# Expert 0 loaded earlier, its splits kept in the projection tiles, and routing in two nearly equal parts

## The chip, the core and the metric

The kernel runs on one core of one Trainium2 chip. The metric is the time of one execution in microseconds (us), as the device takes it. The engines are named as in the profile: PE (TensorE, matrix products), DVE (VectorE), ACT (ScalarE), POOL (GpSimd), and SP, whose queue issues most transfers.

## The reference

Four batches (B) of 576 tokens (S), 8 heads of 64, 512 model columns (DM), 1024 inner columns (FF), 8 experts. It is cut to what is computed:

```python
# attention: each query sees the 64 keys up to itself
scores = where((rel >= 0) & (rel < 64), scale * (q @ k.T), -1e9)
x = softmax(scores) @ v
# gated FFN: projection, a 3-tap filter along the tokens, projection
h = maximum(x @ w_in, 0.0)
conv_out[t] = sum(conv_w[k] * h[t + k - 1] for k in range(3))
x = (h * sigmoid(conv_out)) @ w_out
# mixture of experts, one expert per token
logits = x @ w_gate
local_gate = sigmoid(x @ w_local)
for b, s:
    e = argmax(logits[b, s]) if s == 0 or local_gate[b, s] < 0.5 else prev_e
    p = softmax(logits[b, s])
    out[b, s] = p[e] * (maximum(x[b, s] @ w1[e], 0.0) @ w2[e])
```

A token thus keeps the expert of the token ahead of it when its local gate says so.

## The kernel before

**Exact products.** fp32 data is held as a high and a low part (names ending in H and L, or h and l), and each product is three PE matmuls: high x high, high x low, low x high. The high part is a copy by ACT (`cast`), the low part a subtraction (`rest_of`) on DVE, or on POOL for slot 0.

**Phase 1, the batches.** For each batch `ffn(b)` goes through eight feature tiles (f0 to f7) of 128 columns. 24 matmuls per tile (L345) are evacuated by ACT into `hb`; the filter and gate (L361 to L371) run on POOL, DVE and ACT and leave `gH` and `gL`, the gated features, in a ring. Then `ffn_out(i)` (L384) multiplies each tile of 128 tokens with `wout` (24 matmuls of 512 columns) and stores `y` through SP's queue. The attention of the next batch is mixed between these steps by `mix`, and `share(b)` says how many of its steps may have run after a given number of FFN steps. In this phase a scheduler sets the order of the engines' instructions from a timing model; nothing is reordered by hand.

**The transition.** The last batch's tiles are numbered 13 to 17 (I0 = 13, NT = 18). From `logits_ahead` on, the order of PE, DVE and ACT is written out. `logits_ahead` computes the gate logits of tiles 13 to 17 straight from gH and gL (48 PE matmuls L453 into `psG`, two per feature tile and product), `gate` and `route` find each token's expert, and its rank among that expert's tokens (PE steps L630, L639, L645, L656 to L664, each a round trip to DVE), and `A` is the one-hot matrix of the rank. `slots_of` turns that into slots of 128 tokens of one expert: DVE's products `bm` (L695 to L702), PE's L706, the token indices `gidx`, and the output weights `pslot` (POOL's products `bp` at L745, PE's L749, DVE's reduction L750). `tail()` yields one output matmul at a time, and `ahead(n)` puts n of them (fillers) at a place in the order. Tiles 0 to 12 have been routed in batch 3 already.

**Phase 2, the slots.** 23 slots run without condition, two more under one. Slot t has a gather, `X` (4 transpositions), `MM1` (24 matmuls, L890), `HT` (8 transpositions), `MM2` (24 matmuls, L920), and a scatter of rows from `osb` to `out`. Expert weights come as raw tiles `raw1` and `raw2` (4 each, 512 KB a tile), are split by ACT and DVE (L836, L842), and a load is skipped where the expert stays. Slot 0's x stays on the chip: `X0` takes it from `psX`, which L414 fills. In this kernel the raw tiles and the split tiles (pools `ws`, `ws2`) take the space that `win`, `x` and `h` leave when phase 1 closes, so expert 0's loads (L795, L797) begin after the last L345.

Of the kernel before, what the change touches and what calls it, by code (L numbers as in the profile page):

```python
# [21 lines left out]
def kernel(  # L22
# [29 lines left out]
    RING = 640  # L52
    scale = 1.0 / float(D) ** 0.5
# [39 lines left out]
    if True:  # L93
# [6 lines left out]
        hb = [h_p.tile([P, S + 2], F32, name=f"hb{i}", bufs=1) for i in range(2)]  # L100
# [146 lines left out]
        def stage_AV(b, hp, g):  # L247
            if (b, hp, g) == (b, 0, 0):
                xT[b] = []
            if g == 0:  # L250
                xT[b].append((x_p.tile([P, S], F32R, name="xH"), x_p.tile([P, S], F32R, name="xL")))
# [71 lines left out]
        def ffn(b):  # L323
# [3 lines left out]
            for f in range(KF):  # L327
                if b == 0:
                    if cin:
                        fin.append(conv_in(*cin.pop(0)))  # L330
                        if len(fin) > 1:
                            fin.pop(0)()
                    fin.append(conv_out(f))
                    if f:
                        fin.pop(0)()
# [18 lines left out]
                t = h_p.tile([P, S], F32, name="t", bufs=3)  # L354
# [189 lines left out]
        I0 = (B - 1) * S // P  # L544
        gidx = const.tile([P, TS], I32, name="gidx")
# [15 lines left out]
        def route_init():  # L561
# [4 lines left out]
            def iota(shape, pattern, base, mult, name):  # L566
                ti = r1.tile(shape, I32, name=name + "_i")
# [27 lines left out]
            tl("ohc", [P, NT - I0, E], BF16)  # L595
# [29 lines left out]
        def route(i0, i1):  # L625
# [47 lines left out]
            if i0 == 0:  # L673
                s_ = r1.tile([P, E], F32, name="ohs")
                nc.vector.tensor_reduce(s_, oh.rearrange("p i e -> p e i"), axis=AX.X, op=ALU.add)
                nc.vector.tensor_copy(rt["ohc"], s_.unsqueeze(1).to_broadcast([P, NT - i1, E]))
            nc.vector.tensor_tensor(
                rt["A"][:, g], rl.unsqueeze(2).to_broadcast([P, n, P]), rt["i128"].unsqueeze(1).to_broadcast([P, n, P]), op=ALU.is_equal
            )

        def slots_of():
# [109 lines left out]
    x0_p = ctx.enter_context(tc.tile_pool(name="x0", bufs=1, side="right"))
    raw1 = [raw_p.tile([P, FF], F32, name=f"raw1_{kk}") for kk in range(KD)]
    raw2 = [raw_p.tile([P, 2, DM], F32, name=f"raw2_{kk}") for kk in range(KD)]
    for kk in range(KD):
        nc.sync.dma_start(out=raw1[kk], in_=w1[0, kk * P:(kk + 1) * P, :])  # L795
    for kk in range(KD):
        nc.sync.dma_start(out=raw2[kk], in_=w2[0, kk * 2 * P:(kk + 1) * 2 * P, :].rearrange("(j p) d -> p j d", p=P))  # L797
# [3 lines left out]
    KORD = (3, 0, 1, 2)  # L801
# [10 lines left out]
    def load1(t):  # L812
        for kk in KORD:
# [4 lines left out]
                cond=c,  # L818
# [91 lines left out]
    def MM2(t):  # L910
# [11 lines left out]
        o = s2.tile([P, DM], F32, name="osb")  # L922
# [6 lines left out]
    def start(t):  # L929
        load1(t)  # L930
# [4 lines left out]
    def run(t0, t1):  # L935
# [4 lines left out]
        if t0 + 1 < t1:  # L940
            gather(t0 + 1)
            load1(t0 + 1)
            load2(t0 + 1)
            if t0 == 0:
                split(raw1, w1s, "a", 1, KORD[0:1])
                X0(rt["psX"], 1)
# [56 lines left out]
    with tc.manual_schedule(engines={mybir.EngineType.PE, mybir.EngineType.DVE, mybir.EngineType.Activation}):  # L1003
# [31 lines left out]
        for _ in rest:  # L1035
            pass
# [43 lines left out]
```

## Time and profile before

| | |
|---|---|
| three timed runs | 681.88, 684.84, 686.81 us (median 684.84) |
| the profiled execution | 680.33 us |
| its span | 678.5 us |
| PE busy | 639.7 us, 94% |
| DVE busy | 515.2 us, 76% |
| ACT busy | 449.7 us, 66% |
| POOL busy | 205.2 us, 30% |
| mean granted clock | 0.967 |

The span is the time from the first to the last instruction of the profiled execution. About the first 140 us hold the attention and FFN of batch 0 with the conversion of the weights; batches 1 to 3 run to 335, the transition to 384, the slots to 671, and the last scatter to the end. In the rows, a window is a stretch of the span with the busy time of each engine in it and the number of instructions; the granted clock is 1.00 for 2.4 GHz and 0.50 for 1.2 GHz. In a timeline row the bracket tells how long the engine waited before the instruction, and for what.

### The profile page before, as it was taken

The page shows a single profiled execution, that of the slowest core. Times are in us where ns is not written, and L with a number is a line of the kernel's source. Part 1 is how long each engine was busy: PE and PEld are TensorE (multiplying, and loading weights), DVE is VectorE, ACT ScalarE, POOL GpSimd, SP SyncE. Part 2 cuts the span into 40 slices and gives each one's busy share as a digit, 9 for nine tenths or more (in the row PEclk, how much of TensorE's full clock was granted, in tenths as well). Part 3 has the DMA queues.
Part 4 walks back from the last instruction along what each step waited for, and adds up shares of the span by engine and source line. Part 5 has one row for each costly group of instructions (what it writes and reads, how often), then busy time and mean ns, then how long its engine had stood idle before and what let it go on. Part 6 is the DMA issues. An engine that isn't in the chain of part 4 may idle for free.

```text
span 678.5 us, 13033 instructions
## 1 busy us (share of the span) xinstructions
PE 639.7 (94%) x4379; PEld 555.0 (82%) x4379; DVE 515.2 (76%) x1054; ACT 449.7 (66%) x972; POOL 205.2 (30%) x223
## 2 busy tenths in 40 slices
PE   5688897999999999999979999999999999999994
PEld 4468787899999999999847878888888888888883
DVE  4877999726893467825968659989899899899982
ACT  3575755636784467623433468898889888988972
POOL 5553565301541023432757421121111211211101
PEclk9788999899999999999969999999999999999998
DMA  7867350342234202010141246611451444412760
GB/s 164 210 168 185 95 128 32 76 120 67 68 67 102 79 32 53 12 63 32 60 188 47 64 152 223 241 60 34 156 178 37 165 158 156 161 42 83 238 257 12
DMA packets 91880, 75.75 MB, mean 112 GB/s; under 512 B 72266, under 2 KB 72290, under 8 KB 91812
## 3 DMA queue, kind: packets, MB, share of 16 engines
q1 hardware_dynamic: 87040, 64.11, 31.7%
q0 software_dynamic: 3680, 10.75, 4.7%
q8 instruction: 35, 0.57, 0.4%
q14 instruction: 33, 0.27, 0.1%
q10 hardware_dynamic: 1092, 0.04, 0.1%
HBM read 127.84 MB, written 11.27 MB: 205 GB/s over the span
## 4 chain that ended last, share of the span: by engine, by line
PE 39%; issue 31%; DMA 14%; DVE 11%; POOL 2%; ACT 2%; SPq 1%; POOLq 0%; DVEq 0%; ACTq 0%
PE psM L345 12%; PE psO L384 12%; DMA out_dram<-osb,sidx 10%; PE psA L195 3%; PE psA L261 3%; PE psA L238 2%; POOL xg L861 2%; PE psA L166 2%; DMA raw<-in_moe_w_in_dram 1%; DVE t L362 1%; PE psA L198 1%; DVE lf L469 1%; DVE t L363 1%; DVE lf L467 1%; DMA raw<-in_moe_w_dram 1%
## 5 line engine op out<-in xcount | busy, mean ns | idle before, releaser
L842 DVE TENSOR_TENSOR aL<-raw,aH 128x1024 fp32r<-128x1024 f32 x88 | 102.0, 1220 | 12.0 <-ACT aH L836 12.0
L842 DVE TENSOR_TENSOR bL<-raw,bH 128x1024 fp32r<-128x1024 f32 x84 | 97.3, 1220 | 3.6 <-ACT bH L836 0.9
L924 POOL DMA_INDIRECT out_dram<-osb,sidx x23 | 23.3, 1015 | 231.6 <-ACT osb L923 224.3
L836 ACT ACTIVATE aH<-raw 128x1024 fp32r<-128x1024 f32 x92 | 90.1, 1062 | 0.6 <-DVE gL L371 0.6
L836 ACT ACTIVATE bH<-raw 128x1024 fp32r<-128x1024 f32 x88 | 86.3, 1067 | 0.0
L345 PE MATMUL psM<-xH,winH 128*128 128x288 f32 x256 | 79.8, 312 | 0.1
L345 PE MATMUL psM<-xL,winH 128*128 128x288 f32 x256 | 77.3, 302 | 0.0
L345 PE MATMUL psM<-xH,winL 128*128 128x288 f32 x256 | 76.4, 299 | 0.0
L371 POOL TENSOR_TENSOR gL<-t,gH 128x576 fp32r<-128x576 f32 (+6 forms) x54 | 57.5, 1074 | 57.7 <-ACT gH L370 57.7
L920 PE MATMUL psO<-bH,hh 128*128 128x512 f32 x184 | 74.0, 402 | 0.4 <-ACT hh L907 0.4
L920 PE MATMUL psO<-bL,hh 128*128 128x512 f32 x184 | 72.3, 393 | 0.5 <-DVE bL L842 0.5
L920 PE MATMUL psO<-bH,hl 128*128 128x512 f32 x184 | 72.4, 393 | 0.0
L890 PE MATMUL psH<-aH,xh 128*128 128x512 f32 x176 | 70.9, 403 | 0.0
L890 PE MATMUL psH<-aH,xl 128*128 128x512 f32 x176 | 69.3, 394 | 0.0
L890 PE MATMUL psH<-aL,xh 128*128 128x512 f32 x176 | 69.2, 393 | 0.0
L384 PE MATMUL psO<-woutH,gH 128*128 128x262 f32 (+2 forms) x240 | 63.4, 311 | 1.4 <-ACT gH L370 1.4
L361 POOL TENSOR_SCALAR t<-hb,cw 128x576 f32<-128x576 f32 x31 | 30.4, 980 | 113.2 <-ACT hb L352 100.2
L384 PE MATMUL psO<-woutH,gL 128*128 128x262 f32 (+2 forms) x240 | 62.4, 307 | 0.9 <-POOL gL L371 0.9
L384 PE MATMUL psO<-woutL,gH 128*128 128x262 f32 (+2 forms) x240 | 63.1, 307 | 0.0
L213 ACT ACTIVATE sS<-sS,mx 128x128 f32<-128x128 f32 (+1 forms) x144 | 55.2, 387 | 11.1 <-DVE mx L205 10.9
L345 PEld LDWEIGHTS psM<-xH,winH 128*128 128x128 f32 x256 | 49.0, 191 | 1.0 <-ACT hb L352 0.4
L345 PEld LDWEIGHTS psM<-xL,winH 128*128 128x128 f32 x256 | 48.9, 191 | 0.3
(281 smaller groups left out, 1498.5 us busy)
## 6 DMA issues: line engine op xcount, KB each, us to landing
raw<-in_moe_w_dram SPq DMA_DIRECT2D x180, 512.0 KB
v<-in_v_dram SPq DMA_DIRECT2D x56, 128.0 KB
y_dram<-ysb SPq DMA_DIRECT2D x18, 256.0 KB
kt<-in_k_dram SPq DMA_DIRECT2D x32, 128.0 KB
qt<-in_q_dram SPq DMA_DIRECT2D x32, 128.0 KB
raw<-in_moe_w_in_dram SPq DMA_DIRECT2D x8, 512.0 KB
raw<-in_moe_w_out_dram SPq DMA_DIRECT2D x8, 512.0 KB
raw2e<-in_moe_w_dram SPq DMA_DIRECT2D x4, 512.0 KB
```

The costliest lines, as they stand in the source:

```text
L195: nc.tensor.matmul(ps[:, j * P + lo:(j + 1) * P], qbd[:, c, :], kT[:, k0:W * (c + 1)], start=True, stop=True)
L213: nc.scalar.activation(sS[:, c, lo:P], sS[:, c, lo:P], AF.Exp, scale=-1.0, bias=mx[:, c:c + 1], accum_out=sume[:, c:c + 1],)
L261: nc.tensor.matmul(ps[64 * h:64 * h + 64, W * j:W * j + W], vt[:, h, :], a[0:kk, j, 64 * h:64 * h + 64], start=True, stop=True,)
L345: nc.tensor.matmul(ps[:, 0:HS], wt[:, kk, f * P:(f + 1) * P], xt[:, c0:c0 + HS], start=n == 0, stop=n == 3 * KD - 1,)
L361: e1.tensor_scalar(tt, h1, cw[:, 1, f:f + 1], 0.0, op0=ALU.mult, op1=ALU.add)
L371: e1.tensor_tensor(gL[:, f, r:r + m], t[:, done:done + m], gH[:, f, r:r + m].bitcast(F32), op=ALU.subtract)
L384: nc.tensor.matmul(p_[:, 0:cs.stop - cs.start], gt[:, kk, r:r + P], wt[:, kk, cs], start=n == 0, stop=n == 3 * KF - 1,)
L836: nc.scalar.activation(H_, raws[kk], AF.Copy)
L842: eng.tensor_tensor(L_, raws[kk], H_.bitcast(F32), op=ALU.subtract)
L890: nc.tensor.matmul(ps, a, w[:, g * DM:(g + 1) * DM], start=n == 0, stop=n == 3 * KD - 1)
L920: nc.tensor.matmul(ps, a[:, kk], w[:, kk % 2, :], start=n == 0, stop=n == 3 * KF - 1)
L924: nc.gpsimd.indirect_dma_start(out=out[:, :], out_offset=bass.IndirectOffsetOnAxis(ap=sidx[:, t:t + 1].bitcast(U32), axis=0), in_=o, in_of ...
```

## The change

- `win`, `wout`, `x`, `h` and the ring are kept for the whole kernel. The split weights of the slots live in them by turns: even slots in `win` and `x` (and an end of the ring), odd slots in `wout` and the ring. The pools `ws`, `ws2`, `x0` and the second output buffer `osb` are gone; the staging of a slot's output is `o_v`, one view of `h`. The space so freed takes `raw1` and `raw2`, and expert 0 is loaded at the start of batch 3.
- Tiles 0 to 8 (R0 = 9) are routed at that point, 9 to 17 in the transition (before: 0 to 12 and 13 to 17). The gate of tiles 9 to 12 is computed when the FFN of batch 3 comes to f = 5.
- Slot 0's low parts are made by DVE, behind the index operations of `slots_of`. `norm` and `chosen` (parts of `slots_of` before) run in steps of `route`.
- The fillers have new numbers, and `tail()` first takes tiles 13 and 14 in turn.
- `share(b)` spreads the attention of batches 2 and 3 over 28 steps, 16 of them in the FFN's matmuls.
- At the end HT(22) moves into MM2(21), and the last raw weights use `raw1`.

The core of the diff:

```diff
 def tail():
-    for i in range(I0, NT):
+    first = [ffn_out(i, False, 1) for i in (I0, I0 + 1)]
+    for g in first:
+        for _ in range(3 * (KF - 1)):
+            yield next(g)
+    for g in first:
+        yield from g
+    for i in range(I0 + 2, NT):
...
-        for n in (4, 2, 2, 2, 0):
+        for n in (22, 6, 2, 1, 0):
             next(lg, None)
             ahead(n)
-        split(raw1, w1s, "a", 0, KORD[0:2])
         gate(I0, NT)
-        ahead(8)
-        ks = list(KORD[2:])
-        for _ in route(I0, NT):
-            ahead(5)
-            if ks:
-                split(raw1, w1s, "a", 0, (ks.pop(0),))
         gate_exp(I0, NT)
+        ahead(7)
+        for _, n, f in zip(route(R0, NT), (4, 2, 3), (None, norm, chosen)):
+            if f:
+                f()
+            ahead(n)
         sl = slots_of()
         next(sl)
-        split(raw1, w1s, "a", 0, ks)
         for kk in KORD:
-            ahead(12)
+            ahead(9)
+            cast(raw1, w1s, "a", 0, kk)
+        ahead(2)
+        next(sl)
+        next(sl)
+        for kk in KORD[0:3]:
             cast(raw2, w2s, "b", 0, kk)
-        ahead(12)
-        next(sl)
-        for kk in KORD:
-            rest_of(raw2, w2s, 0, kk)
-        ahead(7)
-        next(sl, None)
+        for kk in KORD[0:3]:
+            rest_of(raw1, w1s, 0, kk)
+        ahead(14)
+        rest_of(raw1, w1s, 0, KORD[3])
         for _ in rest:
             pass
+        X0(rt["psX"], 1)
+        next(sl, None)
...
 def rest_of(raws, store, t, kk):
-    eng = nc.vector if t else nc.gpsimd
-    eng.tensor_tensor(L_, raws[kk], H_.bitcast(F32), op=ALU.subtract)
+    nc.vector.tensor_tensor(L_, raws[kk], H_.bitcast(F32), op=ALU.subtract)
...
 def ffn(b):
             for f in range(KF):
+                if b == B - 1 and f == 5:
+                    gate(R0, I0)
+                    gate_exp(0, I0)
...
 def share(b):
-    n1, n2, na = 4 * KF, 4 * (4 + b % 2), 34
-    if b == 0:
-        return lambda m: 16 * m // n1 if m <= n1 else 16 + (na - 16) * (m - n1) // n2
-    return lambda m: na * m // (n1 + n2)
+    n1, n2, na = 4 * KF, 4 * (4 + b % 2), 34 if b == 0 else 28
+    return lambda m: 16 * m // n1 if m <= n1 else 16 + (na - 16) * (m - n1) // n2
...
 # in run(t0, t1)
+                    split(end2, w2s, "b", t, KORD[0:2])
+                    MM2(t - 1, {8: lambda: HT(t)})
+                    split(end2, w2s, "b", t, KORD[2:4])
```

On DVE the end of batch 3's FFN stands as follows before; the L361 to L365 are the filter's steps of f6 and f7 (f7 in two parts), and A is the first routing part's one-hot matrix.

```order
L668 TENSOR_TENSOR rk<-psR,oh 128x104
L669 TENSOR_REDUCE rf<-rk 128x13
L670 CAST ri<-rf 128x13
L365 SCALAR_TENSOR_TENSOR t<-t,hb_132 128x576
L671 TENSOR_SCALAR rl<-ri 128x13
L672 TENSOR_SCALAR rh<-ri 128x13
L362 SCALAR_TENSOR_TENSOR t<-hb_131,cw,t 128x576
L677 TENSOR_TENSOR A<-rl,i_4053 128x1664
L363 SCALAR_TENSOR_TENSOR t<-hb_131,cw,t 128x576
L361 TENSOR_SCALAR t<-hb_132,cw 128x287
L361 TENSOR_SCALAR t<-hb_132,cw 128x289
```

And on DVE now (the steps have the numbers L370 to L374, and `t` and `hb` are views of h):

```order
L682 TENSOR_SCALAR rh<-ri 128x9
L693 TENSOR_TENSOR A<-rl,i_4017 128x1152
L374 SCALAR_TENSOR_TENSOR h<-h 128x576
L371 SCALAR_TENSOR_TENSOR h<-h,cw 128x576
L372 SCALAR_TENSOR_TENSOR h<-h,cw 128x576
L374 SCALAR_TENSOR_TENSOR h<-h 128x576
L371 SCALAR_TENSOR_TENSOR h<-h,cw 128x576
L372 SCALAR_TENSOR_TENSOR h<-h,cw 128x576
L374 SCALAR_TENSOR_TENSOR h<-h 128x576
L371 SCALAR_TENSOR_TENSOR h<-h,cw 128x576
L372 SCALAR_TENSOR_TENSOR h<-h,cw 128x576
L370 TENSOR_SCALAR h<-h,cw 128x287
```

`A` now has three whole feature tiles between it and the first step of f7 (128x287).

On PE, from the transposition of `key` to the ranks (L384, now L393, are the fillers), before:

```order
L630 MATMUL psR<-ident,key 18x128
L384 MATMUL psO<-woutH,gH 128x512
L384 MATMUL psO<-woutL,gH 128x512
L384 MATMUL psO<-woutH,gL 128x512
L384 MATMUL psO<-woutH,gH 128x512
L384 MATMUL psO<-woutL,gH 128x512
L639 MATMUL psR<-dg,ltri 18x18
L384 MATMUL psO<-woutH,gL 128x512
L384 MATMUL psO<-woutH,gH 128x512
```

and on PE now:

```order
L640 MATMUL psR<-ident,key 18x128
L393 MATMUL psO<-woutH,gL 128x512
L393 MATMUL psO<-woutH,gH 128x512
L393 MATMUL psO<-woutL,gH 128x512
L393 MATMUL psO<-woutH,gL 128x512
L649 MATMUL psR<-dg,ltri 18x18
L393 MATMUL psO<-woutH,gH 128x512
L393 MATMUL psO<-woutL,gH 128x512
L655 MATMUL psR<-ident,cm 128x18
L393 MATMUL psO<-woutH,gL 128x512
L393 MATMUL psO<-woutH,gH 128x512
L393 MATMUL psO<-woutL,gH 128x512
```

Four fillers stand behind L640 where five stood, two behind L649 where five stood, and three before the ranks where five stood.

## Rows read from the trace of the kernel before

**Rows 1.** The page's 40 slices of the span: TensorE busy, and its clock.

```profile
PE   5688897999999999999979999999999999999994
...
PEclk9788999899999999999969999999999999999998
```

**Rows 2.** Windows of the transition: from:to, length, busy by engine, clock, DMA share, GB/s.

```profile
338.87:354.25 15.38, 11.75 (x37) 6.89 (x36) 10.54 (x23) 6.06 (x11) 9.03 (x5) 0.67 0.57 217
354.25:384.00 29.75, 29.47 (x203) 24.64 (x203) 22.75 (x54) 9.46 (x14) 16.73 (x9) 1.00 0.15 52
```

**Rows 3.** The same windows, L384 on PE and PEld alone.

```profile
338.87:354.25 15.38, 8.00 (x18) 4.88 (x18) 0.67 0.57 217
```

**Rows 4.** The same windows, L453 alone.

```profile
335.20:338.87 3.67, 3.63 (x25) 2.15 (x25) 1.00 0.67 232
```

**Rows 5.** Timeline of PE: start, us, engine, line, operation, count, wait.

```profile
341.88 0.76 PE L453 MATMUL psG<-gH,woutH 128*10 128x256 f32 x2 [1.93 <-ACT gH L370]
...
343.97 0.49 PE L453 MATMUL psG<-gL,woutH 128*10 128x384 f32 x1 [0.89 <-POOL gL L371]
...
354.26 0.27 PE L630 MATMUL psR<-ident,key 128*18 128x128 f32 x1 [0.54 <-DVE key L617]
...
355.62 0.21 PE L639 MATMUL psR<-dg,ltri 18*18 18x18 f32 x2
...
357.12 0.23 PE L645 MATMUL psR<-ident,cm 18*128 18x18 f32 x1
...
363.21 0.39 PE L384 MATMUL psO<-woutH,gH 128*128 128x512 f32 x1
363.44 0.39 PE L384 MATMUL psO<-woutL,gH 128*128 128x512 f32 x1
...
382.01 0.82 PE L749 MATMUL psR<-bp,A 128*128 128x75 bf16 x18
...
390.24 0.66 PE L872 MATMUL psX<-ident,xg 128*128 128x128 f32 x4
```

**Rows 6.** Timeline of DVE.

```profile
335.92 2.70 DVE L677 TENSOR_TENSOR A<-rl,i 128x1664 bf16<-128x1664 int32 x1
...
350.23 0.21 DVE L462 COPY L_all<-psG 128x50 f32<-128x50 f32 x1 [2.19 <-PE psG L461]
...
351.21 2.28 DVE L613 TENSOR_TENSOR eq<-eq,w 128x40 f32<-128x40 f32 x1
...
356.07 0.28 DVE L642 TENSOR_SCALAR cm<-cm,cr 18x128 f32<-18x128 f32 x1
...
363.12 2.13 DVE L695 TENSOR_TENSOR hi<-hi,rh 128x18 f32<-128x18 f32 x1
365.28 2.77 DVE L697 TENSOR_TENSOR sl<-hi,i 128x450 bf16<-128x450 f32 x1
...
382.87 0.24 DVE L750 TENSOR_REDUCE pslot<-psR 128x25 f32<-128x75 f32 x1 [1.48 <-PE psR L749]
```

**Rows 7.** Timeline of POOL.

```profile
362.80 10.27 POOL L842 TENSOR_TENSOR bL<-raw,bH 128x1024 fp32r<-128x1024 f32 x4 [2.50 <-ACT bH L836]
...
378.37 3.05 POOL L745 TENSOR_TENSOR bp<-sl,pp 128x450 bf16<-128x450 bf16 x3 [2.30 <-DVE pp L740]
```

**Rows 8.** Timeline of SP.

```profile
382.62 0.34 SPq L431 DMA_DIRECT2D y_dram<-ysb  x1
```

**Rows 9.** Timeline of PE in the last slot.

```profile
664.02 0.50 PE L920 MATMUL psO<-bH,hh 128*128 128x512 f32 x1 [0.39 <-ACT hh L907]
...
666.71 0.50 PE L920 MATMUL psO<-bL,hh 128*128 128x512 f32 x1 [0.55 <-DVE bL L842]
```

**Rows 10.** Windows of batch 0.

```profile
118.00:120.00 2.00, 0.97 (x6) 0.75 (x7) 1.92 (x6) 1.92 (x5) 1.00 (x1) 1.00 0.01 4
...
122.00:124.00 2.00, 2.00 (x17) 1.88 (x18) 2.00 (x5) 1.67 (x3) 0.96 (x1) 0.50 0.44 97
```

**Rows 11.** The chain that ended last, its longest landing of an output.

```profile
639.50 7.44 DMA out_dram<-osb,sidx
```

More of the change, by code (lines that the diff above doesn't have):

```diff
@@ L52 @@
     RING = 640
+    KORD = tuple(range(DM // P))
     scale = 1.0 / float(D) ** 0.5
@@ L99 @@
         gL = ring_p.tile([P, KF, RING], F32R, name="gL")
-        hb = [h_p.tile([P, S + 2], F32, name=f"hb{i}", bufs=1) for i in range(2)]
+        NX = 6
+        xs_t = x_p.tile([P, NX * 2 * S], F32R, name="x")
+        h_t = h_p.tile([P, 2 * (S + 2) + 3 * S], F32, name="h")
+        hb = [h_t[:, i * (S + 2):(i + 1) * (S + 2)] for i in range(2)]
+        tb = [h_t[:, 2 * (S + 2) + i * S:2 * (S + 2) + (i + 1) * S] for i in range(3)]
         qbds = [at1.tile([P, NC, P], F32, name=f"qbd{i}") for i in range(2)]
@@ L250, in stage_AV @@
             if g == 0:
-                xT[b].append((x_p.tile([P, S], F32R, name="xH"), x_p.tile([P, S], F32R, name="xL")))
+                n = (b * NP + hp) % NX * 2
+                xT[b].append([xs_t[:, (n + j) * S:(n + j + 1) * S] for j in range(2)])
             xH, xL = xT[b][hp]
@@ L778 @@
                 p1a.close()
+                raw_p = ctx.enter_context(tc.tile_pool(name="raw", bufs=1, side="right"))
+                raw1 = [raw_p.tile([P, FF], F32, name=f"raw1_{kk}") for kk in range(KD)]
+                raw2 = [raw_p.tile([P, 2, DM], F32, name=f"raw2_{kk}") for kk in range(KD)]
+                x0_q = raw_p.tile([P, 2 * P], F32R, name="x0q")
+                for kk in KORD:
+                    nc.sync.dma_start(out=raw1[kk], in_=w1[0, kk * P:(kk + 1) * P, :])
+                for kk in KORD:
+                    nc.sync.dma_start(out=raw2[kk], in_=w2[0, kk * 2 * P:(kk + 1) * 2 * P, :].rearrange("(j p) d -> p j d", p=P))
@@ L791, with pieces @@
[L791 to L797, printed above, removed]
+    def pieces(t, n):
+        f = t if len(t.shape) == 2 else t.rearrange("p a b -> p (a b)")
+        return [f[:, i * FF:(i + 1) * FF] for i in range(n)]
@@ new lines @@
+    pw, pg, px = pieces(woutH, 4) + pieces(woutL, 4), pieces(gH, 5) + pieces(gL, 5), pieces(xs_t, 6)
+    pairs = {
+        (0, "a"): [(winH[:, kk, :], winL[:, kk, :]) for kk in range(KD)],
+        (0, "b"): list(zip(px[0::2], px[1::2])),
+        (1, "a"): list(zip(pw[0:4], pw[4:8])),
+        (1, "b"): list(zip(pg[0:4], pg[5:9])),
+    }
+    pairs[0, "b"].insert(KORD[-1], (pg[4], pg[9]))
+    x0v = [xs_t[:, 6 * FF + i * 2 * P:6 * FF + (i + 1) * 2 * P] for i in range(3)] + [x0_q]
+    x0v = [t.rearrange("p (k x) -> p k x", x=P) for t in x0v]
@@ L800 @@
+    hs_v = [h_t[:, i * FF:(i + 1) * FF] for i in range(2)]
+    o_v = h_t[:, 2 * FF:2 * FF + DM]
     NG = FF // DM
-    KORD = (3, 0, 1, 2)
     regs = {}
@@ L852, in X0 @@
     def X0(ps, half):
-        xh, xl = (x0_p.tile([P, KD // 2, P], F32R, name=f"x0{x}{half}") for x in "HL")
+        xh, xl = x0v[2 * half:2 * half + 2]
         nc.scalar.activation(xh, ps[:, 0:KD // 2], AF.Copy)
@@ L881, in MM1 @@
         ws = w1s.pop(t)
-        h = hs_[t] = s2.tile([P, FF], F32, name="hs")
+        h = hs_[t] = hs_v[t % 2]
         for g in range(NG):
@@ L921, in MM2 @@
                 n += 1
-        o = s2.tile([P, DM], F32, name="osb")
+                if n in mids:
+                    mids[n]()
+        o = o_v
         nc.scalar.activation(o, ps, AF.Copy, scale=pslot[:, t:t + 1])
@@ L929, in start @@
     def start(t):
-        load1(t)
+        load1(t, True)
         load2(t, raw2)
@@ L939, in run @@
             X(t0)
[L940 to L946, printed above, removed]
-                split(raw1, w1s, "a", 1, KORD[1:4])
-            else:
-                split(raw1, w1s, "a", t0 + 1)
-            if t0 + 2 < t1:
-                load1(t0 + 2)
-        end2 = raw2
+        else:
+            gather(1)
+            load1(1)
+            cast(raw2, w2s, "b", 0, KORD[3])
+            for kk in KORD:
+                rest_of(raw2, w2s, 0, kk)
+            load2(1)
+        end2 = [t.rearrange("p (j d) -> p j d", j=2) for t in raw1]
         for t in range(t0, t1):
-            last = t > t0 and t == t1 - 1
             if t > t0 + 1:
                 split(raw2, w2s, "b", t - 1)
-                if not last:
+                if t + 1 < t1:
                     load2(t)
```

98 lines of the change are left out of this document (51 added, 47 removed).

## The prediction

> **What bounds the kernel now.** I read the page's forty slices first (17 us each). From the eighth on TensorE shows 9 nearly everywhere; the one dip with a fallen clock after the start is the slice that begins at 339 us, 7 tenths busy at 6 tenths of full clock [rows 1]. The slots behind it are packed, so time can come from that dip, from the last slot, and from little else. The windows name it: 338.87 to 354.25 us is 15.38 us long, TensorE busy 11.75 us at a mean clock of 0.67; the 29.75 us behind it hold 29.47 us of work at full clock [rows 2].
>
> What is really computed in the dip? 37 instructions [rows 2]: 18 output matmuls of L384 [rows 3], five small transpositions of L461, and so 14 logit matmuls of L453. At full clock two L384 start 0.23 us apart (363.21 and 363.44) [rows 5], and 25 L453 took 3.63 us, 0.145 each [rows 4]. 18 x 0.23 + 14 x 0.145 = 6.2 us, and I allow 0.5 us for the transpositions and the restarts: 6.7. So 15.38 - 6.7 = 8.7 us are lost. Waits show as 1.93 and 0.89 us for the last feature tile's gH and gL and 0.54 us for `key`, 3.4 together [rows 5]. The rest, some 5.3 us, is clock: a mean of 0.67 between levels 1.0 and 0.5 means that 66% of 15.38 us, 10.1 us, ran at 1.2 GHz, which does 5.1 us less work. TensorE had waited twice just before. The two ways to the number agree.
>
> Why did f7's gH come late? On VectorE the 2.70 us comparison `A` (L677, 128x1664) stands between steps of the convolution of tiles f6 and f7 [rows 6]; L453 for f6 and f7 stands on TensorE ahead of nearly all the output matmuls that could fill the time.
>
> **The change, part by part.**
>
> *Routing of tiles 0 to 8 instead of 0 to 12.* `A` becomes 128x1152, 1.9 us by size, and stands three feature tiles earlier (the fence on VectorE), where 3 of TensorE's feature tiles lie between it and the end. Before, TensorE's last wait for gL ends at 343.97 and the last L345 at about 335.3: 8.7 us. Without the 2.7 us that chain takes some 6.
>
> *The order on TensorE.* 30 instead of 13 of the 48 logit matmuls run inside the FFN, then 6, 22 output matmuls, 6, 6 and 6. The 22 fillers are 22 x 0.23 = 5.1 us, with the 12 logit matmuls ahead of f7's own part and 6 more fillers 8.2 us. Chain at 6 (7 if POOL and VectorE hinder each other) against 8.2: no wait here, so no reason for the clock to fall. The whole 8.7 us goes, also the 0.54 for `key`, which I charge anew below.
>
> *The raw weights of expert 0*, 4 MB, start at batch 3's beginning instead of after the FFN, and have all of that FFN to land. *Slot 0's split* leaves POOL (10.27 us for four pieces) [rows 7] for VectorE. I cost both at nothing: the split stands behind the routing's indices, and VectorE's chain from the ranks to the index product (L706, now L737) gets 38 fillers, 8.7 us, as cover. That chain took about 14 us, but 2.13 of it was L695 and 2.77 L697 [rows 6], with two more of L697's size, all beside POOL's split; with 0.2 and some 0.6 for these four it is 6 to 7 us, the longer `A` of the second part included. If it stayed at 14, 5 us would be lost here.
>
> *What is next to wait: the routing steps.* They have fewer fillers. Each is a round trip TensorE, VectorE, TensorE:
> - logits to `key`: 7 fillers, 1.6 us. VectorE's chain took from 350.23 [rows 6] to 354.26 [rows 5], 4.0 us, of which L613 had 2.28 us with POOL at work; with 0.2 in its place 2.0. Wait 0.4 to 0.5.
> - `key` (354.26) to the next product (355.62) was 1.36 us [rows 5] with 5 fillers; 4 are 0.92. Wait 0.4.
> - to `cm`: VectorE's last step there began at 356.07 and took 0.28 [rows 6], so 0.75 us from 355.62; 2 fillers are 0.46. Wait 0.2 to 0.3.
> - to the ranks: 0.95 us by the steps behind 357.12 [rows 5], and ahead of them now stand the three steps of `norm`, some 0.75 us if each takes about what L642 took, of which 0.4 stand in the way; 3 fillers are 0.7. Wait 0.6.
>
> Together 1.7 us. The bounds: 0 (if VectorE's latencies are as they were with POOL idle, and fillers take 0.25) and 3 (if steps of 2 us come back).
>
> *Slot weights (`pslot`)*: the 18 small matmuls L749, now L774, started at 382.01 and `pslot`'s reduction on VectorE at 382.87, 0.24 us long [rows 5, 6]. Before, 12 transpositions (L414) lay between it and MM1(0). Now MM1's first matmul stands directly behind, and waits for the reduction because both use one PSUM bank: 382.87 + 0.24 + 0.1 - (382.01 + 0.66) = 0.5, with the queue of VectorE 0.7. Bounds 0 and 2 (a 1.22 us split in front).
>
> *The last y store* goes out on SP's queue behind three reloads of raw tiles, which wait for VectorE's splits; before, it left at 382.62 and X(1) read its rows at 390.24 [rows 5, 8]; I count no slack there. Behind it in line are the gather of slot 1, X(1) and all that follows. VectorE's three splits are 3 x 1.2 us, TensorE's remaining fillers about as long. I take 0.5, between 0 and 0.9.
>
> Here a rule bears. VectorE's L695 took 2.13 us for 18 elements [rows 6] while POOL ran slot 0's subtractions of 2.6 us [rows 7]; the neighbours of that size take 0.2. The Trainium skill, "SBUF — State Buffer", section "Who interferes with whom", says that a VectorE instruction with two SBUF inputs and a GpSimd instruction that reads SBUF exclude each other for a whole instruction, whoever starts first; the trace agrees, and the rule speaks for taking the split off POOL, but against where it goes.
>
> *The end.* HT(22) moves into MM2(21), and two weight pieces are cast earlier. The waits of 0.39 and 0.55 us [rows 9] go, and the restarts behind them, which I estimate at 0.5 from the two matmuls' 0.50 us each where 0.39 is usual [rows 5, 9] and a pause before each: 1.5. The second half of the split may now come 0.3 late. Gain 1.2, bounds 0.5 and 1.5.
>
> *No price*: conditions on loads, KORD, tiles as views of larger tiles, one `o_v` for two output buffers (a rival).
>
> **Sum**: 8.7 - (1.7 + 0.7 + 0.5) + 1.2 = 7.0 us. The profiled execution, 680.33 us, would be 673.3. It is the fastest of four; the timed three are 681.88, 684.84 and 686.81, and the mean of the four 683.5. Taking 684, nearer their median, I get **677.0**, 1.1% under the median of 684.84. One per cent, 678.0, is about what a measurement of this kernel tells from no change.
>
> **Rivals.**
> - *The routing waits don't come* (fillers cover them): 8.7 + 1.2 = 9.9 us, 674. For it: before, three of the four steps showed no wait [rows 5]. Against it: one to three fillers fewer at each.
> - *The clock falls once more* in the routing, where TensorE would wait four times within 6 us. In batch 0 a stretch of 0.97 us busy in 2 us was followed by one at 0.50 [rows 10]. It takes back between 1.0 us (one such row) and 5.1 (as in the dip): 678 to 682, say 680.5. Against it: the waits here are 0.2 to 0.6 us each.
> - *Exclusion beside `bp`*: POOL's three `bp` products, 3.05 us [rows 7], now run while VectorE splits slot 0's tiles. If they alternate strictly, the third split, SP's reloads, the y store and X(1) come some 2 us later than with none instead of 0.5. Gain 5.5: 678.5. This is the outcome by the skill's rule named above.
> - *The change doesn't do what it says*: the f7 chain still ends after the fillers, since the scheduler's order of batch 3 also gives VectorE more `gate` steps ahead of it. Then 2.8 us of waits and the clock come back: gain 0 to 2, 682.5.
> - *Re-dealt attention*: batches 1 and 2 now have 16 of 28 steps in the FFN's matmuls and 12 in the output's. If that makes waits as batch 0 has them, at least 1.0 + 1.0 us in the two rows [rows 10] and, estimated, as much in their neighbours, two batches cost 8: 685.
> - *Slower: one output buffer.* The ACT copy of slot t waits until slot t-1's rows have landed; transpositions that stand behind it on ACT wait too. A landing took up to 7.44 us [rows 11], a slot 48 x 0.23 = 11.0 us and its transpositions. It decides from about 11 us after the copy; 1 us over that, 22 times, gives 677 + 22 = 699. Against it: 3 us of room in the worst row.
>
> **How the numbers follow.** Forecast 0.48 (its own spread 673.5 to 680), no waits 0.09, clock 0.16, exclusion 0.10, not doing what it says 0.07, attention 0.06, output buffer 0.04. Beyond 1%: 0.31 of the forecast's 0.48, all of the second, a fifth of the clock and 0.03 of the exclusion: near 0.47. Slower: the buffer and a little of the attention, 0.05. The range runs from 672.0 (9.9 us off a base of 682) to 683.5, which leaves out the attention, the buffer, and about a tenth of the rest.
>
> **What the profile of the changed kernel would show.** Right: no slice with a PEclk under 9 between 140 us and the end; no wait for gH or gL behind the last FFN matmul; four short waits of 0.2 to 0.6 us at the L640, L649, L655 and L666 steps; a wait for VectorE of some 0.7 us at the first L925; PE's last slot without idle time. Wrong: a stretch at 0.5 between 335 and 385 us; waits in 140 to 335 us; ACT's L960 held by out_dram; X(1) over a microsecond late. Most of all the prediction falls if the clock's 5 us don't come back.

## The result and the profile after

The changed kernel takes 675.4 us (median of four executions, 673.35 to 676.7), the kernel before 683.36 us (median of four, 681.62 to 686.81): a ratio of 0.9885, 95% interval 0.9844 to 0.9926. The forecast was 677.0.

The page's slices after the change; the first line is TensorE busy, the second its granted clock:

```profile
PE   5688898999999999999999999999999999999995
...
PEclk9787988899999999999999999999999999999998
```

The dip of [rows 1] is gone: from the ninth slice to the last but one both lines show 9 throughout. Windows of the transition (columns as in [rows 2]):

```profile
341.00:350.00 9.00, 8.13 (x40) 6.07 (x38) 7.74 (x14) 3.42 (x9) 3.06 (x3) 1.00 0.00 0
350.00:358.00 8.00, 7.79 (x50) 4.80 (x48) 5.15 (x24) 0.83 (x2) 0.00 (x0) 1.00 0.00 0
358.00:367.00 9.00, 9.00 (x50) 7.22 (x46) 5.58 (x19) 5.12 (x7) 0.00 (x0) 1.00 0.25 90
```

What is left of waits on TensorE, in its timeline:

```profile
342.22 0.34 PE L462 MATMUL psG<-gL,woutH 128*10 128x384 f32 x1 [0.87 <-POOL gL L380]
...
354.27 0.27 PE L640 MATMUL psR<-ident,key 128*18 128x128 f32 x1
...
355.61 0.21 PE L649 MATMUL psR<-dg,ltri 18*18 18x18 f32 x2
...
357.62 0.21 PE L666 MATMUL psR<-oh,ltrib 128*128 128x72 bf16 x1
...
367.14 0.63 PE L737 MATMUL psR<-bm,A 128*128 128x50 bf16 x18
...
380.26 0.50 PE L925 MATMUL psH<-winH,x 128*128 128x512 f32 x1 [0.43 <-DVE pslot L775]
...
386.33 0.60 PE L907 MATMUL psX<-ident,xg 128*128 128x128 f32 x4
...
387.18 0.66 PE L940 MATMUL psX<-ident,h 128*128 128x128 f32 x4 [0.25 <-ACT h L929]
```

The routing steps (L640 to L666), which answer to [rows 5], have no wait in their brackets. VectorE's and POOL's timelines beside them:

```profile
357.33 0.23 DVE L659 TENSOR_TENSOR oh<-ki,i 128x72 bf16<-128x72 int32 x1
...
362.27 0.18 DVE L726 TENSOR_TENSOR hi<-hi,rh 128x18 f32<-128x18 f32 x1
362.49 0.63 DVE L728 TENSOR_TENSOR sl<-hi,i 128x450 bf16<-128x450 f32 x1
...
363.69 0.34 DVE L733 TENSOR_SCALAR bm<-sl,pcol 128x450 bf16<-128x450 bf16 x1
...
372.65 4.23 DVE L877 TENSOR_TENSOR winL<-raw,winH 128x1024 fp32r<-128x1024 f32 x3
...
379.98 0.23 DVE L775 TENSOR_REDUCE pslot<-psR 128x25 f32<-128x75 f32 x1
```

```profile
340.11 2.06 POOL L380 TENSOR_TENSOR gL<-h,gH 128x192 fp32r<-128x192 f32 x2
...
370.71 3.96 POOL L770 TENSOR_TENSOR bp<-sl,pp 128x450 bf16<-128x450 bf16 x3 [0.73 <-DVE pp L765]
```

The sum for 18 elements takes 0.18 us where [rows 6] has 2.13, the first 450-element product 0.63 instead of 2.77.

Which feature tile TensorE waits for can be read from the engine that makes its gL: POOL for every tile up to f6, VectorE for f7, the last. First the kernel before, then the changed one:

```profile
341.91 2.01 POOL L371 TENSOR_TENSOR gL<-t,gH 128x192 fp32r<-128x192 f32 x2 [5.04 <-ACT gH L370]
344.16 1.05 DVE L371 TENSOR_TENSOR gL<-t,gH 128x192 fp32r<-128x192 f32 x3
345.65 0.73 PE L453 MATMUL psG<-gH,woutH 128*10 128x256 f32 x2
```

```profile
344.77 1.89 POOL L380 TENSOR_TENSOR gL<-h,gH 128x192 fp32r<-128x192 f32 x2 [2.61 <-ACT gH L379]
347.85 0.46 PE L462 MATMUL psG<-gH,woutH 128*10 128x256 f32 x2
348.89 0.46 DVE L380 TENSOR_TENSOR gL<-h,gH 128x289 fp32r<-128x289 f32 x1 [0.51 <-ACT gH L379]
350.12 0.45 PE L462 MATMUL psG<-gH,woutH 128*10 128x256 f32 x2
```

Before, POOL finished f6's gL at 343.92, and the longer waits of [rows 5] (until 341.88 and 343.97) are for f6. VectorE finished f7's at 345.21, and TensorE came to f7 at 345.65 without a wait. Counted from the start of the last FFN matmul (335.12 before, 340.66 now), f6's gL took 8.8 us before and 6.0 now, f7's 10.1 and 8.7.

**One table for all kernels.** To compare executions I cut each trace at starts of the same matmuls. P: from the first instruction to the 222nd FFN matmul, ahead of which no kernel here differs in its order; A: from there to the first matmul of slot 0; B: to the first of MM2(21); C: to the last matmul. What follows the start of the last takes 7.9 to 8.0 us in all. In the profiled execution of the kernel before, for example, A, B, C and the last matmul start at 161.20, 384.00, 657.12 and 670.55 us. The ratios in the table are to the kernel before as it was timed beside each run (medians of 681.3 to 683.4 us).

| kernel | timed, median us | ratio to before (95%) | P | A | B | C |
|---|---|---|---|---|---|---|
| before | 683.36 | 1 | 161.20 | 222.80 | 273.12 | 13.43 |
| changed | 675.40 | 0.9885 (0.9844 to 0.9926) | 163.44 | 216.82 | 274.46 | 12.03 |
| e1, old fillers | 680.85 | 0.9966 (0.9928 to 1.0004) | 162.78 | 221.66 | 274.48 | 12.03 |
| e2, fillers alone | 684.48 | 1.0029 (0.9992 to 1.0067) | 161.26 | 226.53 | 273.17 | 13.43 |
| e3, old cut | 673.95 | 0.9873 (0.9786 to 0.9959) | 159.66 | 217.22 | 274.70 | 12.03 |
| e4, split on POOL | 679.96 | 0.9956 (0.9918 to 0.9993) | 159.34 | 223.25 | 275.06 | 12.03 |
| e5, old end | 675.93, one run | | 162.08 | 216.84 | 274.45 | 12.68 |
| e6, old share | 673.27, one run | | 160.94 | 216.01 | 274.46 | 12.03 |
| e7, late load | 674.42, one run | | 161.22 | 216.85 | 274.47 | 12.03 |
| e8, no new waits | 673.69 | 0.9876 (0.9831 to 0.9921) | 161.49 | 216.05 | 274.45 | 12.03 |
| e9, order and split | 674.22 | 0.9898 (0.9865 to 0.9932) | 163.74 | 214.91 | 273.19 | 13.43 |
| e10, fillers ahead | 679.45 | 0.9965 (0.9941 to 0.9990) | 158.69 | 220.54 | 274.43 | 12.03 |
| e11, tiles swapped | 677.58, one run | | 161.14 | 220.48 | 274.14 | 12.05 |
| e12, order, split, end | 673.52 | 0.9870 (0.9830 to 0.9909) | 161.08 | 214.56 | 273.16 | 13.33 |

A, B and C repeat within some 0.05 us where the code is the same (B of changed, e1, e5 to e8: 274.45 to 274.48). P varies by 5 us although TensorE's order in it is the same. That most of the spread of the timed runs lies there too is likely, but each kernel has one trace, so it is not shown. Effects under 3 us are read from A, B and C. By them the change is worth 5.98 in A, -1.34 in B and 1.40 in C: 6.0 us. The medians' difference, 8.0 us, holds the luck of P besides.

### The profile page after: what moved, and what is told of

The parts are those of the page before. It is cut to its first block, busy times and chain, and to the rows that moved or that the text cites. A ratio compares the mean times of both kernels' runs of the same rounds, so it can differ in the third digit from the quotient of the medians.

```text
span 674.7 us, 13065 instructions
## 1 busy us (share of the span) xinstructions
PE 639.6 (95%) x4383; PEld 556.1 (82%) x4383; DVE 517.0 (77%) x1069; ACT 449.4 (67%) x972; POOL 187.4 (28%) x215
## 4 chain that ended last, share of the span: by engine, by line
PE 34%; issue 31%; DMA 14%; DVE 14%; ACT 2%; POOL 2%; SPq 1%; POOLq 0%; DVEq 0%; ACTq 0%
PE psO L393 13%; DMA out_dram<-h,sidx 12%; PE psM L354 8%; PE psA L200 3%; PE psA L267 3%; DVE h L372 2%; DVE h L371 2%; DMA raw<-in_moe_w_in_dram 1%; PE psA L243 1%; DVE lf L478 1%; DVE lf L477 1%; ACT sS L218 1%; DVE sS L228 1%; DVE h L374 1%; DVE lf L476 1%
## 5 line engine op out<-in xcount | busy, mean ns | idle before, releaser
L354 PE MATMUL psM<-x,winH 128*128 128x288 f32 x512 | 112.0, 308 | 0.4 <-DVE x L273 0.2
L354 PEld LDWEIGHTS psM<-x,winH 128*128 128x128 f32 x512 | 83.6, 193 | 2.3 <-ACT h L361 0.8
L354 PE MATMUL psM<-x,winL 128*128 128x288 f32 x256 | 77.0, 301 | 0.0
L380 POOL TENSOR_TENSOR gL<-h,gH 128x576 fp32r<-128x576 f32 (+6 forms) x54 | 58.9, 1102 | 38.2 <-ACT gH L379 38.1
L877 DVE TENSOR_TENSOR gL<-raw,gH 128x1024 fp32r<-128x1024 f32 x56 | 65.6, 1220 | 2.2 <-ACT gH L872 0.7
L393 PE MATMUL psO<-woutH,gH 128*128 128x262 f32 (+2 forms) x240 | 64.6, 310 | 0.0
L393 PE MATMUL psO<-woutH,gL 128*128 128x262 f32 (+2 forms) x240 | 62.1, 304 | 0.9 <-POOL gL L380 0.9
L393 PE MATMUL psO<-woutL,gH 128*128 128x262 f32 (+2 forms) x240 | 62.8, 301 | 0.0
L370 POOL TENSOR_SCALAR h<-h,cw 128x576 f32<-128x576 f32 x31 | 29.2, 943 | 114.3 <-ACT h L361 107.0
L877 DVE TENSOR_TENSOR winL<-raw,winH 128x1024 fp32r<-128x1024 f32 x48 | 56.4, 1235 | 3.6 <-ACT winH L872 3.6
L872 ACT ACTIVATE gH<-raw 128x1024 fp32r<-128x1024 f32 x56 | 55.7, 1066 | 0.0
L877 DVE TENSOR_TENSOR woutL<-raw,woutH 128x1024 fp32r<-128x1024 f32 x44 | 51.0, 1221 | 2.8 <-ACT woutH L872 2.8
L354 PEld LDWEIGHTS psM<-x,winL 128*128 128x128 f32 x256 | 49.1, 192 | 0.1
L872 ACT ACTIVATE winH<-raw 128x1024 fp32r<-128x1024 f32 x48 | 47.0, 1061 | 0.0
L393 PEld LDWEIGHTS psO<-woutH,gL 128*128 128x128 f32 x240 | 40.9, 189 | 2.5 <-POOL gL L380 1.1
```

What stands on the lines that cost most here:

```text
L354: nc.tensor.matmul(ps[:, 0:HS], wt[:, kk, f * P:(f + 1) * P], xt[:, c0:c0 + HS], start=n == 0, stop=n == 3 * KD - 1,)
L370: e1.tensor_scalar(tt, h1, cw[:, 1, f:f + 1], 0.0, op0=ALU.mult, op1=ALU.add)
L380: e1.tensor_tensor(gL[:, f, r:r + m], t[:, done:done + m], gH[:, f, r:r + m].bitcast(F32), op=ALU.subtract)
L393: nc.tensor.matmul(p_[:, 0:cs.stop - cs.start], gt[:, kk, r:r + P], wt[:, kk, cs], start=n == 0, stop=n == 3 * KF - 1,)
L872: nc.scalar.activation(H_, raws[kk], AF.Copy)
L877: nc.vector.tensor_tensor(L_, raws[kk], H_.bitcast(F32), op=ALU.subtract)
```

## The experiments

The theory: TensorE lost 8.7 us because it had nothing to do while the filter's chain of the last feature tiles ran, and its clock then fell; fillers there bring them back, as long as VectorE's routing is quick. Rivals: the early load brings it, or the moved comparison `A`, or the order of the fillers alone.

### e1: the old fillers

```diff
-        for n in (22, 6, 2, 1, 0):
+        for n in (4, 2, 2, 2, 0):
...
-            ahead(9)
+            ahead(n)  # 15, 14, 14, 14
```

> The changed kernel, but with the filler numbers of before behind the logit matmuls (4, 2, 2, 2, 0 instead of 22, 6, 2, 1, 0); the 21 fillers go ahead of the index product L737. Theory (TensorE had nothing to do behind the last feature tile's chain, and the fillers put there cover it): the chain still ends some 8.4 us after the last FFN matmul, 12 logit matmuls and 10 fillers cover about 4, so waits of 4 to 5 us for gH and gL come back, the granted clock falls to 0.5 for some us behind them, and the time goes to 680 to 684. Rival (the early load and the split on VectorE bring the gain): within 2 us of the changed kernel, 674 to 677.

Its waits of TensorE (engine, line, waited for, us, times, longest) and two windows:

```profile
PE psG L462 <- POOL gL L380: 1.8, 2, 0.9
PE psG L462 <- ACT gH L379: 1.6, 2, 1.0
```

```profile
346.00:348.00 2.00, 1.61 (x6) 0.70 (x6) 1.69 (x5) 1.16 (x4) 0.00 (x0) 0.65 0.00 0
348.00:350.00 2.00, 1.78 (x6) 1.06 (x7) 0.96 (x3) 0.16 (x1) 0.00 (x0) 0.50 0.00 0
```

A is 4.84 us longer than in the changed kernel: 2.5 more of waits (3.4 instead of 0.9), and the half clock behind them. The theory's, though its waits of 4 to 5 us were put too high; they stand at f5 (0.9), f6 (1.0 and 0.9) and f7 (0.6). With the early load, the split on VectorE and the new cut all in place, 81% of A's gain is gone.

### e2: the fillers alone, on the kernel before

```diff
-        for n in (4, 2, 2, 2, 0):
+        for n in (22, 6, 2, 1, 0):
...
         for kk in KORD:
-            ahead(12)
+            ahead(8)
             cast(raw2, w2s, "b", 0, kk)
-        ahead(12)
+        ahead(7)
```

and `tail()` with tiles 13 and 14 in turn.

> The kernel before with the new filler numbers behind the logit matmuls and tiles 13 and 14 in turn, nothing else. Theory: no wait for f7's gH and gL, and no fallen clock there (8.7 us), but with slot 0's split still on POOL the VectorE chain to the index product L706 stays some 14 us against 39 fillers, 9 us, so some 5 us of wait come up at L706, perhaps with the clock: 678 to 683. Rival (the order alone brings it all): 675 to 677, no wait over 1 us at L706.

The waits in the transition, three windows and VectorE's steps:

```profile
PE psR L706 <- DVE bm L702: 3.7, 1, 3.7
PE psR L630 <- DVE key L617: 3.6, 1, 3.6
```

```profile
350.00:354.00 4.00, 0.83 (x4) 0.37 (x2) 3.93 (x5) 0.00 (x0) 3.56 (x2) 0.90 0.00 0
354.00:358.00 4.00, 3.62 (x10) 2.50 (x11) 1.55 (x7) 0.18 (x1) 0.00 (x0) 0.50 0.00 0
...
376.00:380.00 4.00, 4.00 (x34) 3.81 (x34) 3.07 (x18) 0.60 (x1) 1.26 (x1) 0.64 0.20 71
```

```profile
349.29 2.02 DVE L612 TENSOR_TENSOR eq<-L_all,mx 128x40 f32<-128x40 f32 x1
351.35 2.27 DVE L613 TENSOR_TENSOR eq<-eq,w 128x40 f32<-128x40 f32 x1
```

The dip at the filter's chain is gone as forecast, and A is 3.7 us longer than before all the same: the wait turned up at `key` and at the index product, 7.3 us in two, and the clock fell behind both. The timed median, 684.48, is above the theory's 678 to 683. At `key` I had not expected it; POOL's 2.3 us subtractions run at that moment, and two comparisons of 40 elements take 2.0 and 2.3 us.

### e3: the old cut of the routing

```diff
-        R0 = 2 * S // P
+        R0 = I0
...
-                    gate(R0, I0)
```

> The changed kernel, but with the routing cut at tile 13 as before, so that the comparison of 128x1664 stands on VectorE between the filter steps of f6 again. Theory (the fillers cover the chain with about 1 us to spare): the chain ends some 2 us later, waits of 1 to 2 us, clock stays, 676 to 678. Rival (moving the comparison is what frees TensorE): the dip with the fallen clock is back, 680 or more.

`A` is 2.71 us long again, but the scheduler put it between the steps of f5, one tile earlier than before, and not of f6 as I had expected. TensorE waits 0.43 us for f5's gH and 0.67 for its gL; the clock stays. A is 0.40 longer than in the changed kernel, so the theory's way, and cheaper than it said: the changed kernel's own wait of 0.87 is not added to these but replaced. The cut as a whole is worth 0.40 us in A here and 0.24 in B, where X(1) waits 0.5 us for its gather. The timed median, 673.95, lies under the theory's range. What the comparison costs at f6 with this order is seen in e9, where it stands as before and no wait for gH or gL shows.

### e4: slot 0's split on POOL

```diff
+        eng = nc.vector if t else nc.gpsimd
-        nc.vector.tensor_tensor(L_, raws[kk], H_.bitcast(F32), op=ALU.subtract)
+        eng.tensor_tensor(L_, raws[kk], H_.bitcast(F32), op=ALU.subtract)
```

> The changed kernel with slot 0's low parts on POOL again. Theory (POOL's subtractions hold up VectorE's routing steps): the 450-element steps of some 0.6 us and the short sum ahead of them take 2 to 3 us again, the chain to L737 loses its 3 us of room and TensorE waits there 1 to 4 us: 677 to 680. Rival (no matter who splits): within 1 us, 675 to 676.

```profile
PE psR L737 <- DVE bm L733: 4.8, 1, 4.8
```

```profile
363.00:368.00 5.00, 0.17 (x1) 1.00 0.00 0
368.00:372.00 4.00, 3.99 (x27) 0.57 0.10 17
```

(The windows here show TensorE alone.) L726, the sum of 18 elements, takes 1.97 us and L728 2.72. The room of 3 us at L737 is gone, TensorE stands 4.8 us and then runs 4 us at a mean of 0.57. A is 6.43 us longer, all of its gain, and B 0.60. The wait is the theory's, larger than its 1 to 4, and the fallen clock on top I had left out.

### e5, e6 and e7: the end, the spread, the load

```diff
# e5
-                    MM2(t - 1, {8: lambda: HT(t)})
+                    MM2(t - 1)
+                    HT(t)
# e6
-            n1, n2, na = 4 * KF, 4 * (4 + b % 2), 34 if b == 0 else 28
+            n1, n2, na = 4 * KF, 4 * (4 + b % 2), 34
...
+            return lambda m: na * m // (n1 + n2)  # for b > 0
# e7: the eight dma_starts of raw1 and raw2 from batch 3's start to behind the last mix
```

> The changed kernel, but HT(22) stands behind MM2(21) as before. Theory: the waits for hh, and for a weight piece, come back in the last slot: from the first matmul of MM2(21) to the last of all 1.0 to 1.6 us more than in the changed kernel. Rival (the wait is only moved to the last weight piece): under 0.3 us.

C is 0.65 longer, less than the theory's 1.0 to 1.6, with the wait of 0.4 for hh back, but none for a weight piece. So HT's place is about half of C's 1.40. For the other half the order of the pieces is the likely cause (e12).

> The changed kernel with the old spread of the attention over batches 1 and 2. Theory: TensorE is full from 163 us to the last FFN matmul in either spread, so that stretch is the same within 0.7 us. Rival (the new spread takes out waits or makes some): 2 us or more of difference, and a row of waits.

By the code, the attention in e6 overwrites tiles of x that the FFN of the batch before still reads, and its values are not the reference's: with six x tiles kept in turn, the new spread is needed and not a choice. The stretch from the 222nd to the last FFN matmul is 177.24 us where the changed kernel has 177.22. The theory holds there; A's 0.81 us less comes behind it, as the wait of 0.87 for gL isn't there in this run. Why the old spread removes that wait I did not trace.

> The changed kernel with expert 0's eight loads issued behind the last FFN matmul instead of at the start of batch 3. Theory: nothing before the splits, some 18 us later, needs them, so the stretch from the last FFN matmul to the first slot matmul is the same within 0.7 us. Rival (the load at the dip was part of the loss): 2 us or more longer.

A is 216.85 against 216.82. The early load by itself brings nothing.

### e8 and e10: the remaining waits

```diff
# e8
+        ahead(5)
         for n in (22, 6, 2, 1, 0):
...
-            ahead(9)
+            ahead(n)  # 8, 8, 8, 7
...
+        next(sl, None)
         for _ in rest:
             pass
         X0(rt["psX"], 1)
-        next(sl, None)
# e10, as e8 but
-                if kk >= KF - 2:
+                if kk >= KF - 3:
                     yield
...
+        for n in (5, 18, 7, 2, 1, 0):
...
+            ahead(n)  # 8, 8, 7, 7
```

> The changed kernel with 5 fillers taken from those ahead of L737 and put ahead of the last 18 logit matmuls, and with the small product L774 ahead of the last six transpositions L423 instead of behind them. Theory: the waits of 0.87 us for gL and of 0.43 us for pslot go, and nothing else comes up, since VectorE is done with L737's input 3 us early: 1.0 to 1.5 us less from the last FFN matmul to the first slot matmul, 674. Rival (the waits come up again at the next step, the gather of slot 1 or f7's chain): under 0.4 us.

0.77 less in A, between the theory's 1.0 to 1.5 and the rival's 0.4. The wait for pslot is gone, so 0.43 of it; for gL 0.8 us of wait are left, now in two parts, since the fillers ended up ahead of the last FFN matmuls and put those off too.

> The changed kernel with fillers ahead of the logit matmuls of f5, f6 and f7 (5, 18, 7, 2, 1, 0) and 6 fewer ahead of L737, and with L774 ahead of the last transpositions. Theory: no wait for gL nor for pslot is left, 215.3 to 215.8 us from the 222nd FFN matmul to the first slot matmul (changed kernel 216.8, the run with fillers ahead of all 18 logit matmuls 216.05). Rival (f7's chain is late again, because a filler ahead of f5's part also delays the last FFN matmul): a wait of 0.5 us or more for f7's gH or gL, 216 or more.

```profile
PE psR L774 <- POOL bp L770: 3.6, 1, 3.6
```

The wait for gL is gone, as expected, and A is 3.7 us longer than in the changed kernel through a slip of mine: my numbers place four fillers fewer in all, which put L774 in front of 37 output matmuls and six transpositions that are ahead of it in e8, when POOL's `bp` isn't ready yet. The granted clock is 0.50 from 368.0 to 371.4 us, behind that wait, and this adds to the 3.6 us. Neither theory spoke of that. It shows how little room there is: the same move gains 0.4 us or loses 3.6.

### e9 and e12: the two parts together on the kernel before

e9 is the kernel before with the transition and the first slots written as in the diff (fillers, casts, slot 0's low parts on VectorE behind the indices, slot 1's split behind HT(0)), and `norm` and `chosen` where they were:

```diff
-        eng = nc.vector if t else nc.gpsimd
-        eng.tensor_tensor(L_, raws[kk], H_.bitcast(F32), op=ALU.subtract)
+        nc.vector.tensor_tensor(L_, raws[kk], H_.bitcast(F32), op=ALU.subtract)
...
-        for n in (4, 2, 2, 2, 0):
+        for n in (22, 6, 2, 1, 0):
...
+        for _, n in zip(route(I0, NT), (4, 2, 3)):
+            ahead(n)
```

> The kernel before with two parts of the change together: the new order of the fillers (and of slot 0's split in the transition and the first slots), and slot 0's low parts on VectorE behind the indices. The tiles, the pools, the load behind the FFN, the routing cut at tile 13, the spread of the attention and the end stay as before. Theory (the order of the fillers and the split off POOL bring the gain only together): from the 222nd FFN matmul to the first slot matmul 217 to 218.5 us, where before has 222.8, the changed kernel 216.8, and the fillers alone 226.5; no fallen clock. Rival (the early load, the cut or the spread is needed as well): 220 or more, with a wait over 2 us or a fallen clock.

```profile
PE psH L889 <- DVE pslot L750: 0.6, 1, 0.6
...
PE psX L904 <- ACT hs L893: 0.3, 1, 0.3
PE psR L639 <- DVE dg L636: 0.2, 1, 0.2
```

```profile
351.77 0.20 DVE L612 TENSOR_TENSOR eq<-L_all,mx 128x40 f32<-128x40 f32 x1
352.00 0.20 DVE L613 TENSOR_TENSOR eq<-eq,w 128x40 f32<-128x40 f32 x1
```

A is 214.91 us, 7.9 less than before and 1.9 less than in the changed kernel; better than the theory's own range. The comparisons that took 2.0 and 2.3 us in e2 take 0.20. With -3.7 for the order alone and +7.9 for both, neither the early load, nor the kept tiles, the cut or the spread is needed for the gain. In A and B together e9 is 3.18 us shorter than the changed kernel: what it leaves out costs more there than it brings. Of the 1.91 us in A 0.84 is idle time on TensorE (1.63 us in the changed kernel, 0.79 here). The rest is matmul distance: without idle time A is 215.2 to 215.3 us in the changed kernel, e3, e6 and e7, and 214.1 here, 214.2 in e12. So neither the cut nor the spread nor the load makes it alone; the tiles' places are the likely cause, as in B (e11), but no run tests them in A.

e12 adds e8's place of L774 (here L749) and HT(22) inside MM2(21).

> The kernel before with the new order and the split on VectorE (as in the run of these two), and in addition L749 ahead of the last six transpositions and HT(22) inside MM2(21). It leaves out the early load, the tiles of the projections as places of the split weights, the new cut and the new spread. Theory: 214.3 to 214.6 us from the 222nd FFN matmul to the first slot matmul (214.91 with the wait for pslot), 273.2 to the first matmul of MM2(21) as before (changed kernel 274.46), 12.0 to 12.3 behind that: 3 to 4 us less than the changed kernel in the trace, and 670 to 674 us timed. Rival (what was left out buys something that shows with the rest): not faster than the changed kernel in the trace.

```profile
PE psO L919 <- DVE bL L841: 0.8, 1, 0.8
PE psO L919 <- ACT bH L836: 0.3, 1, 0.3
```

A (214.56) and B (273.16) are as expected; C is 13.33, not 12.0 to 12.3, so that the whole gain is under the theory's 3 to 4 us. I had kept KORD as (3, 0, 1, 2), and MM2 reads pieces 0, 1, 2, 3: the two pieces split early are 3 and 0, so piece 1, wanted after six matmuls, is late. Over A, B and C e12 takes 501.05 us where the changed kernel takes 503.31. That it is 2.3 us faster is what the traces say; the timed medians, 673.52 and 675.40, lie the same way with intervals that overlap.

### e11: the weights' places swapped

```diff
-        (1, "a"): list(zip(pw[0:4], pw[4:8])),
-        (1, "b"): list(zip(pg[0:4], pg[5:9])),
+        (1, "a"): list(zip(pg[0:4], pg[5:9])),
+        (1, "b"): list(zip(pw[0:4], pw[4:8])),
```

> As the run with fillers ahead, but in odd slots the weights of MM1 lie in the ring and those of MM2 in wout, instead of the other way round. It looks at the 1.34 us that the slots of the changed kernel take more than before, all of it in the distance of matmuls without any wait: in odd slots MM1, reading wout, takes 5.40 us where before has 5.31, while MM2, reading the ring, has 5.32 as before. If the place of the weights sets the distance, the 0.09 us move to MM2 and MM1 comes down to 5.31 or so; the slots as a whole stay about as long. If it is the role (MM1 beside whatever else runs then), MM1 stays at 5.40.

From the first to the last of 24 matmuls, mean over slots 4 to 19, in us (from their starts):

| | MM1 even | MM1 odd | MM2 even | MM2 odd |
|---|---|---|---|---|
| before | 5.450 | 5.311 | 5.443 | 5.313 |
| changed | 5.461 | 5.400 | 5.454 | 5.322 |
| e11 | 5.447 | 5.328 | 5.436 | 5.404 |

The 0.09 us went with wout from MM1 to MM2: the place sets it. The even slots, whose places stayed, came out 0.014 and 0.018 us shorter; why is open. (e11 was built on e10 and shares its misplaced L774.)

## Why the prediction was right, step by step

- **The dip, 8.7 us.** Right in size, wrong in the tile. The waits of 1.93 and 0.89 us were for f6 and not for the last feature tile; `A` stands between f6's own steps. (Two of the 14 logit matmuls counted in the dip belong to the stretch ahead of it, 0.3 us.) Those waits and the half clock are gone in the changed kernel, and e9, which has little else in A, gains 7.9 with 0.6 and 0.2 us of new waits.
- **The chain at some 6 us against a cover of 8.2.** The 8.7 us that this was worked out from are f6's, and f6's chain did take 6.0. The cover was counted up to f7's part, and f7's chain took 8.7. It did no harm, but with luck: TensorE came to f6's part at 347.85, 1.2 us after its gL, and to f7's at 350.12, only 0.77 us after 349.35, and the unforeseen wait of 0.87 us for f5 had made it that late.
- **Cover for VectorE's chain to the index product.** Right, and the step on which all depends. From the ranks to the end of `bm` VectorE took 6.4 us (forecast 6 to 7) and was done at 364.0; L737 began at 367.14. I priced the failure of that cover at 5 us; e2 has 3.7 there, e4 4.8.
- **Four routing waits, 1.7 us.** Mis-sized: no bracket at any of the four; the groups by line give 0.1 us each for L649 and L666. I had counted 0.23 us per filler and nothing for the small matmuls and the switches between, and these are likely what covers the rest: from L640 to L649 it is 1.34 us with four fillers where before has 1.36 with five [rows 5]. The rival without these waits was right in this.
- **Not seen: 0.87 us for gL behind the last FFN matmul.** The logit matmuls there begin with f5's, whose gL from POOL was ready at 342.17. I had looked at the last tile alone.
- **pslot 0.7:** 0.43. **X(1) 0.5:** the y store left 2.3 us ahead of MM1(0), where before it left 1.4 ahead, so no delay; the wait of 0.25 next to it is for ACT's copy of h.
- **The end, 1.2:** 1.40, 0.65 of it by HT's place (e5).
- **"No price" for the tiles:** wrong by 1.34 us, 0.06 per slot, in the distance of matmuls.
- **The sum, 7.0:** 6.0 by the traces, 8.0 by the medians. That it comes so near is partly luck. The small waits were priced some 2.5 us too high (routing 1.5, X(1) 0.5, pslot 0.3, the end 0.2); against that stand 0.87 for f5, 1.34 in B and about 1.1 of matmul distance in A that were not priced.
- **Rivals.** The clock did not fall after waits of 0.2 to 0.9 us; it did after 3.4 in four pieces (e1), 3.6 and 3.7 (e2), 4.8 (e4) and 3.6 (e10). The chain did not end behind the fillers (0.77 us of room), and the new spread of the attention costs nothing up to the last FFN matmul (e6). Exclusion beside `bp`: the rule of the Trainium skill, "SBUF — State Buffer", "Who interferes with whom", shows between `bp` and the splits. The third `bp` began 0.17 us behind the first split and took 1.84 us, where the two ahead of it took 0.93 and 0.94; the second split began behind that `bp` and took 1.96 us instead of 1.21. So it costs 0.75 us and not 2, because two of the three `bp` were over before VectorE came to the splits; in e2 and e4 steps held up by POOL cost what the change gains. The output buffer: B shows no wait.

## What to carry to other kernels

A filler order and the helper engine's load belong together: the order alone lost 3.7 us in A, everything but the order (e1) brought 1.1, the order with the split on VectorE 7.9. When a stall is filled, follow the next round trip on the same engine pair, and look whether its short steps are at their own length or at that of another engine's instruction. Cut the trace at identical matmuls before comparing executions: a spread of 5 us in a stretch that nothing touched hid what 0.05 us tell behind it.

## What the runs showed of the hardware

- A VectorE step that meets a running POOL subtraction can be held until that ends. In e2 two comparisons of 40 elements take 2.02 and 2.27 us and end at 351.31 and 353.62, POOL's subtractions at 351.26 and 353.56; with POOL idle they take 0.20 us (e9). It is not only steps with two inputs: in e4 a cast of 8 elements takes 2.32 us and ends at 361.20, POOL's subtraction at 361.17.
- The distance of two 512-column matmuls at full clock depends on where the weights lie: 24 of them took 5.31 to 5.46 us with no wait and the same clock, and the 0.09 us of one place went with it when its role was swapped (e11). What about the place does it is open.
- The 222nd FFN matmul, ahead of which TensorE's order is the same in all kernels here, began between 158.7 and 163.7 us; the clock up to there averaged 0.91 (e10) to 0.89 (e9), with TensorE busy 132.6 and 138.0 us.
